# An FFT-and-GeGLU kernel: the opening of the first image in two residue halves

## The chip, the cores and the metric

The kernel runs on one core of a Trainium2 chip. The metric is the device time of one execution in microseconds (us).

## The reference

For eight images `x[b]` of 3008 x 256 the reference takes the real part of a Fourier transform along both axes and feeds each of the 24064 rows to a gated feed-forward block:

```
X = np.fft.fft(np.fft.fft(x, axis=1), axis=2).real
g = X @ w_gate;  gelu = 0.5 * g * (1 + erf(g / sqrt(2)))
out = (gelu * (X @ w_val)) @ w_out        # 256 -> 1536 -> 256
```

## The kernel before

**Numbers of the transform.** The 3008 rows are 64 x 47. For each image the kernel folds the channels (`fold_x`), multiplies by a 64-point table `G` (`a_step`, 12 of them, two of the 24 `jj` each), copies the results to `S1`, sends `S1` through DRAM to get another order on the partitions (`z_write`, `z_read`, tile `Ap`), and multiplies by 47-point tables `TP`, `TQ`, `T0P`, `T0Q` (`b_steps(b, eo, q)`: `eo` is the even or odd channel part, `q` one of four groups of eight of the 32 residues `g`). The result `Y` holds the image as columns, 1505 of them, for the even and the odd channel part. The channel transform itself is folded into the weights: `gen_w` multiplies the cast weights (`cast_w`) with a 256-point table `CW` and gives `WE`, `WOP` and `WOM` (`WOP` with a sign).

**The feed-forward part.** It runs in units. A unit is one block of 128 of the 1536 hidden channels (`fc`, twelve of them) for one chunk of columns; `CH` gives three chunks an image: columns 1024 to 1504 first (481), then 0 to 511, then 512 to 1023. An image has 36 units, and there are 288. In a unit TensorE does `val_even(u)`, `gate_minus(u-1)`, `gate_plus(u)`, `val_odd(u-1)`, six matmuls in all; ScalarE does two Gelus (`glm`, `glp`); VectorE multiplies (`plus`, and in `val_odd`). The first chunk of the first image (units 0 to 11) is of another kind than the rest (`kind` gives 0): its two products are both made by VectorE, straight from PSUM. From unit 12 on VectorE uses a row `nq` (`n_first` for image 0) and GpSimd takes part of the products. The second layer (`l2_steps`, tile `Wo_sb`) of a chunk is spread over the next chunk's units, eight matmuls a unit, so units 0 to 11 have none.

**What fills units 0 to 11.** Behind each unit's matmuls stand, in the order of the program: `gen_w` of the weight blocks 512 and 1024 (`extra`, units 0 to 7), `gen_wn` (unit 7), and `a_step` of the next image (`a_first`: step 0 in unit 4, 1 in unit 5, 2 and 3 in unit 8, two a unit in 9 to 11). They write PSUM tiles `ps_o` and `ps_d`, of which there is one buffer each; a new user waits until the copy of the one before it has been made. VectorE copies `a_step` 0, 3, 5, 7 and 9 of image 1 and makes `WOM`; ScalarE copies the others and makes `WE` and `WOP`.

**Order.** Each engine works in the order in which the program is written (`_InOrder`); nothing is moved by a scheduler. DMAs of the opening are issued by SyncE's queue, in order too. In the opening, `warm(n)` are matmuls whose result nobody reads, and `gate` is a small read that the last eight of them wait for.

**Opening, before.** Load x of image 0; build `G`; for each third of x fold, four `a_step`s, `z_write`; three `z_read`s; the tables `T`; `gen_w` of block 0; all eight `b_steps` of image 0; then unit 0.

Of the kernel before, what the change touches and what calls it, by code (L numbers as in the profile page):

```python
# [37 lines left out]
def kernel(  # L38
# [27 lines left out]
    NJ = 48  # L66
# [6 lines left out]
    CH = [(1024, NCOL - 1024), (0, 512), (512, 512)]  # L73
    MID = 24
# [26 lines left out]
    lone = const_pool.tile([128, NFC], BF16)  # L101

# [92 lines left out]
    def z_tile():  # L195
        return dram.tile([HJ, 128, C], BF16, tag="z", bufs=2, name="z")
# [50 lines left out]
    def cols_t():  # L247
        f4, f8, f16 = (col_q[:, i : i + 1] for i in range(3))
        vec.tensor_scalar(col_q, col_q, MAGIC, None, op0=ALU.add)
        vec.tensor_scalar(col_q, col_q, MAGIC, None, op0=ALU.subtract)  # L250
        vec.scalar_tensor_tensor(col_t, f4, -4.0, col_p, op0=ALU.mult, op1=ALU.add)
        vec.scalar_tensor_tensor(col_bot, f8, -2.0, f4, op0=ALU.mult, op1=ALU.add)
        vec.scalar_tensor_tensor(f8, f16, -2.0, f8, op0=ALU.mult, op1=ALU.add)
        vec.scalar_tensor_tensor(col_j, col_t, 8.0, f16, op0=ALU.mult, op1=ALU.add)
        vec.scalar_tensor_tensor(col_j, f8, 24.0, col_j, op0=ALU.mult, op1=ALU.add)
        vec.tensor_scalar(col_j, col_j, 1.0 / N2, None, op0=ALU.mult)
        for o, b0 in ((0, 0.25), (2 * N2, 0.0)):
            vec.tensor_scalar(
                _sub(quat, [[1, 2 * N2]], o), _sub(col_bot, [[0, 2 * N2]], 0),
                0.25, b0, op0=ALU.mult, op1=ALU.add)  # L260
        vec.tensor_scalar(col_k, col_t, 3.0, None, op0=ALU.is_lt)
        vec.tensor_scalar(col_w, col_k, -TWO_PI, None, op0=ALU.mult)
        vec.tensor_tensor(col_bot, col_bot, col_k, op=ALU.mult)
        vec.tensor_tensor(col_top, col_k, col_bot, op=ALU.subtract)

    TO = 4 * N2
    iota(_sub(rowt, [[2 * N2, 2], [1, 2 * N2]], 0), [[0, 2], [1, 2 * N2]], 0, 0)
    iota(_sub(rowt, [[NJ, 2], [1, MID]], TO), [[0, 2], [1, MID]], 0, 0)
    iota(_sub(rowt, [[NJ, 2], [1, MID - 1]], TO + MID), [[0, 2], [1, MID - 1]], 1, 0)
    pool.memset(_sub(rowt, [[NJ, 2]], TO + NJ - 1), 0.0)  # L270
    pool.memset(_sub(quat, [[1, NJ]], TO), 0.25)
    pool.memset(_sub(quat, [[1, NJ]], TO + NJ), 0.0)
    TG = TO + 2 * NJ
    iota(_sub(rowt, [[NG, 2], [1, NG]], TG), [[0, 2], [-11, NG]], 0, 0)
    pool.memset(_sub(quat, [[1, NG]], TG), 0.25)
    pool.memset(_sub(quat, [[1, NG]], TG + NG), 0.5)
# [59 lines left out]
    def sin_g(i):  # L336
        for h in range(2):
            act.activation(
                _sub(G, [[128, 8], [1, 64]], i * 8 * 128 + h * 64),
                _sub(reds[i], [[64, 8], [1, 64]], 0), AF.Sin, scale=col_h[h][:, :])  # L340

    def turn_g():
        for r, to, of, n, sign in ((0, 0, 0, 16, 1.0), (2, 2, 2, 16, -1.0), (1, 1, 33, 8, 1.0),
                                   (1, 33, 1, 8, -1.0), (3, 3, 35, 8, -1.0), (3, 35, 3, 8, 1.0)):
            pat = [[128, 8], [64, 2], [4, n]]
            act.activation(_sub(G, pat, 16 * 128 + to), _sub(G, pat, of), AF.Copy, scale=sign)
# [44 lines left out]
    def cast_w(f0):  # L391
        big = work.tile([128, 2, NCH, 512], BF16, tag="ev" if f0 == 1024 else "dv", bufs=2, name="wb")
        for i in (1, 0):
            wb[(f0, i)] = big[:, i, :, :]
            pool.tensor_copy(wb[(f0, i)], wst[0][:, i, :, f0 : f0 + 512])

    def gen_w(f0, i, eo, bank):
# [6 lines left out]
        if eo == 0:  # L404
            on_half(ps, act.activation(WE[:, i, fs], ps, AF.Copy))
        else:
            on_half(ps, act.activation(WOP[:, i, fs], ps, AF.Copy))
            on_half(ps, vec.tensor_scalar(
                WOM[:, i, fs], ps, col_m, None, op0=ALU.mult))

# [21 lines left out]
    def n_turn(b):  # L432
        pool.tensor_tensor(
            NA[:, :, :], _sub(Ap, [[0, 2], [C, NG]], 128), TB[:, :, :], op=ALU.mult)
# [46 lines left out]
    def z_write(b, j0, nj, eng=sync):  # L481
        if "z" not in st[b]:
            st[b]["z"] = z_tile()
        z, S1 = st[b]["z"], st[b]["S1"]
        dst = ap_replace(
            z[0:1, 0, :], ap=[[C, 128], [128 * C, nj], [1, C]], offset=z[j0, 0:1, :].offset)
        eng.dma_start(out=dst, in_=_sub(S1, [[C, nj], [1, C]], j0 * C))

    def z_read(b, third):
        z = st[b]["z"]  # L490
        src = ap_replace(
            z[0:1, 0, :], ap=[[NG * C, 32], [1, NG * C]], offset=z[8 * third, 0:1, :].offset)
        p_step = Ap[:, :, :].ap[0][0]
        dst = ap_replace(
            Ap[:, :, :], ap=[[4 * p_step, 32], [1, NG * C]],
            offset=Ap[:, :, :].offset + third * p_step)
        sync.dma_start(out=dst, in_=src)

    def b_steps(b, eo, q):
# [3 lines left out]
        def mm(gi, m1):  # L503
            def run():
                if "ps" not in box:
                    box["ps"] = ((ps_o, ps_d, ps_vh, ps_vh) if eo else (ps_vh, ps_g) * 2)[q]() \
                        if b == 0 else ps_d()
                ps = box["ps"]
                g = 8 * q + gi
                w = _sub(Ap, [[1, 1 if m1 else 128]], g * C + eo * 128)  # L510
# [4 lines left out]
                if g == 0:  # L515
                    t = T0P if even else T0Q
                    keep((pe.matmul(
                        ps[r, 0:N2], w, t[:, 0:N2], start=True, stop=True)))
                    keep(pe.matmul(ps[r, 8 * N2 : 8 * N2 + 1], w, t[:, N2 : N2 + 1],
                                         start=True, stop=True))  # L520
# [13 lines left out]
        def evac_top():  # L534
            ps = box["ps"]
            if Ys[b] is None:
                Ys[b] = Y_tile()
            copy(
                _sub(Ys[b], [[32, MID], [1, 8]], eo * YW + 8 * q),
                _sub(ps, [[1, MID], [N2, 8]], 0))  # L540

        def evac_rest():
            if Ys[b] is None:
                Ys[b] = Y_tile()
            ps, Y, g0 = box["ps"], Ys[b], 8 * q
            n2 = N2 - MID
            f = 1 if q == 0 else 0
            copy(
                _sub(Y, [[32, n2], [1, 8 - f]], eo * YW + 32 * MID + g0 + f - 1),
                _sub(ps, [[1, n2], [N2, 8 - f]], MID + f * N2))  # L550
            if q == 0:
                copy(
                    _sub(Y, [[32, n2]], eo * YW + 32 * MID + 31), ps[:, MID:N2])
                copy(
                    _sub(Y, [[1, 1]], eo * YW + NCOL - 1), ps[:, 8 * N2 : 8 * N2 + 1])

        steps = [mm(gi, False) for gi in range(8)]
        if eo == 1 and b == 0:
            steps += [mm(gi, True) for gi in range(8)]
        def evac():  # L560
            evac_rest()
            evac_top()

        return steps, evac, evac_top, evac_rest


# [11 lines left out]
    def open_unit(u):  # L578
# [3 lines left out]
        c0, n = CH[ci]  # L582
# [82 lines left out]

    def windows(b, ci):
        h = hs[(b, ci)]
        c0, n = CH[ci]
# [8 lines left out]
        if len(blocks) % 4:  # L677
# [4 lines left out]
            pool.tensor_copy(lone, h[:, :, 960:961])  # L682
# [6 lines left out]
    def l2_steps(b, ci):  # L689
# [49 lines left out]

        def store_pair(pair, t, queues):  # L740
            ns = len(pair)
            for q in range(4):
# [23 lines left out]
    for i in (1, 0):  # L766
        load_w(0, i)
    phase_g(0)
    phase_g(1)
    cols_c()  # L770
# [3 lines left out]
    pool.tensor_copy(col_k, _sub(reds[1], [[1, 1]], 0))  # L774
    for i in range(3):
# [3 lines left out]
        else:  # L779
            for t in range(NCH):  # L780
                phase_c(t)
        for k in range(4 * i, 4 * i + 4):
            a_step(0, k)
            if i == 0 and k == 3:
                z_write(0, 0, 8)
            elif i and k % 2:
                z_write(0, 2 * k - 2, 4)
        warm((5, 2, 10)[i])
    z_read(0, 0)
    z_read(0, 1)  # L790
    gate = work.tile([128, 128], BF16, tag="gate", bufs=1, name="gate")
    sync.dma_start(out=gate[:, :], in_=ap_replace(
        st[0]["z"][0:1, 0, :], ap=[[C, 128], [1, 128]], offset=st[0]["z"][0:1, 0, :].offset))
    z_read(0, 2)
    for i in (1, 0):
        load_w(512, i)
    load_x(1, 0)
    for i in (1, 0):
        load_w(1024, i)
    load_x(1, 1)  # L800
    load_x(1, 2)
    reduce_c()
    cols_t()
    pt = phase_t()
    sin_c()
    cast_w(0)
# [3 lines left out]
    gen_w(0, 0, 0, ps_g)  # L810
    gen_w(0, 0, 1, ps_vh)
    act.activation(col_f[:, :], col_p[:, :], AF.Gelu)
    warm(4)
    warm(8, gate[:, :])
    later_evacs = []
    for eo in range(2):
        for q in range(4):
            steps, evac, evac_top, evac_rest = b_steps(0, eo, q)
            for s in steps:
                s()  # L820
            if eo:
                evac_rest()
                later_evacs.append(evac_top)
            else:
                evac()
    cast_w(512)
    load_wo()
    extra = {1: [lambda: cast_w(1024)], 13: [gen_tf]}
    for n, turn in ((0, (ps_o, ps_d, ps_o, ps_d)), (1, (ps_o, ps_o, ps_d, ps_o))):
        for j, bank in enumerate(turn):  # L830
            extra.setdefault(4 * n + j, []).append(
# [15 lines left out]
    plan = [first | evens, later | evens]  # L847
    l2q, few = [], False
    for u in range(NU + 2):
# [4 lines left out]
        if u < NU:  # L854
# [4 lines left out]
            if b + 1 < B:  # L859
                for what in plan[min(b, 1)].get(i, ()):  # L860
# [7 lines left out]
                    fills += st[b + 1]["cur"][0][lo:hi]  # L868
# [13 lines left out]
        if u == 0:  # L882
# [8 lines left out]
            n_first(0)  # L891
# [21 lines left out]
        if tail:  # L913
            tail()
        if 0 < u <= NU:
# [66 lines left out]
```

## Time and profile before

| | us |
|---|---|
| median of 3 runs (range) | 631.35 (629.58 to 631.91) |
| the profiled execution: time, span | 629.75, 627.6 |
| TensorE, busy in the span | 606.0 |
| first `a_step` matmul | 8.88 |
| first `b_steps` matmul of image 0 | 25.34 |
| first matmul of unit 0 | 28.60 |
| first matmul of unit 12 | 51.62 |

A row of the timeline gives start, duration, engine, line, operation, the tile written `<-` the tiles read with their shapes, and in brackets how long the engine had been idle and what ended that. PE is TensorE, PEld its weight loads, DVE VectorE, ACT ScalarE, POOL GpSimd, SP SyncE. All instructions carry line L25, a helper's, so they are told apart by their tiles. A matmul row's duration holds its way through the array; the distance from one start to the next is what a matmul costs in a row of them.

### The profile page before, as it was taken

What the parts mean: (1) busy time and instruction counts of PE and PEld (TensorE: products, weight loads), DVE (VectorE), ACT (ScalarE), POOL (GpSimd) and SP (SyncE); (2) the same over time, 40 slices, a digit from 0 to 9 for tenths busy, and PEclk for the clock granted to TensorE, in tenths of its full rate; (3) what the DMA queues carried; (4) which work ended last, traced back from release to release, by engine and by line L of the source; (5) the groups of instructions that cost most, each with busy time, mean ns of one, the idle gap of its engine ahead of it and who ended that gap; (6) DMA issues with size and microseconds to landing.
All of it is one profiled execution on the core that took longest, in us unless ns stands there. A gap on an engine that the chain in (4) does not pass through costs nothing.

```text
span 627.6 us, 12916 instructions
## 1 busy us (share of the span) xinstructions
PE 606.0 (97%) x4522; PEld 402.0 (64%) x4580; DVE 541.5 (86%) x654; ACT 471.8 (75%) x956; POOL 449.7 (72%) x480
## 2 busy tenths in 40 slices
PE   3899999999999999999999999999999999999997
PEld 2445666766666666766667666666667666666665
DVE  7688988898888998888988898889898898999991
ACT  8687778877788777877778777887778777766662
POOL 8296987769868789687787788687885555556552
PEclk9999999999999999999999999999999999999999
DMA  8997523653237512574246533366223612222113
GB/s 311 348 283 234 153 64 113 173 185 98 76 101 218 194 49 74 177 223 121 51 119 173 190 103 74 104 208 204 56 60 93 194 45 50 60 50 52 39 47 85
DMA packets 65458, 82.39 MB, mean 131 GB/s; under 512 B 8298, under 2 KB 58986, under 8 KB 62578
## 3 DMA queue, kind: packets, MB, share of 16 engines
q1 hardware_dynamic: 63682, 80.65, 42.4%
q0 software_dynamic: 1552, 0.79, 0.9%
q8 instruction: 36, 0.59, 0.4%
q14 instruction: 28, 0.23, 0.1%
q10 hardware_dynamic: 160, 0.13, 0.1%
HBM read 45.08 MB, written 37.25 MB: 131 GB/s over the span
## 4 chain that ended last, share of the span: by engine, by line
PE 91%; DMA 3%; DVE 3%; ACT 1%; issue 1%; POOL 0%; SPq 0%; ACTq 0%; DVEq 0%; POOLq 0%
PE ps_o L25 38%; PE ps_g L25 28%; PE ps_v L25 19%; PE ps_d L25 6%; DMA xin<-in_x_dram 3%; DVE h L25 1%; DVE S L25 0%; DMA z<-S 0%; ACT glp L25 0%; DVE xf L25 0%; ACT glm L25 0%; ACT S L25 0%; POOL xf L25 0%; SPq L25 0%; DVE WOM L25 0%
## 5 line engine op out<-in xcount | busy, mean ns | idle before, releaser
L25 POOL TENSOR_TENSOR h<-glm,dv 128x1024 bf16<-128x1024 bf16 (+1 forms) x138 | 290.9, 2108 | 153.2 <-DVE dv L25 110.0
L25 PE MATMUL ps_o<-Wo_sb,h 128*128 128x256 bf16 x2136 | 277.7, 272 | 0.5 <-DVE S L25 0.3
L25 DVE SCALAR_TENSOR_TENSOR ev<-nq,WN,ps_v 128x512 f32<-128x512 bf16 (+1 forms) x276 | 202.6, 734 | 62.3 <-PE ps_v L25 43.5
L25 ACT ACTIVATE glm<-ps_g 128x512 bf16<-128x512 f32 (+1 forms) x288 | 169.4, 588 | 110.0 <-PE ps_g L25 70.8
L25 PEld LDWEIGHTS <-h 128*128 128x128 bf16 x2208 | 210.8, 97 | 54.6 <-issue 0.9
L25 ACT ACTIVATE glp<-ps_g 128x512 bf16<-128x512 f32 (+1 forms) x288 | 169.9, 590 | 9.9 <-PE ps_g L25 0.3
L25 DVE TENSOR_TENSOR h<-glp,ps_v 128x1024 bf16<-128x1024 bf16 (+2 forms) x150 | 172.9, 1153 | 4.9 <-ACT glp L25 2.7
L25 DVE SCALAR_TENSOR_TENSOR dv<-ev,ps_v 128x1024 f32<-128x1024 f32 (+1 forms) x138 | 164.8, 1194 | 0.0
L25 POOL TENSOR_TENSOR xf<-xin 128x254 bf16<-128x254 f32 x168 | 118.3, 726 | 1.8 <-DMA xin<-in_x_dram 1.8
L25 PE MATMUL ps_g<-Y,WOM 128*128 128x512 bf16 (+1 forms) x288 | 107.7, 374 | 0.3
L25 PE MATMUL ps_v<-Y,WOP 128*128 128x512 bf16 (+1 forms) x288 | 107.7, 374 | 0.0
L25 PE MATMUL ps_v<-Y,WE 128*128 128x512 bf16 (+1 forms) x282 | 105.7, 375 | 0.1
L25 PE MATMUL ps_g<-Y,WOP 128*128 128x512 bf16 (+1 forms) x278 | 103.9, 374 | 1.7
L25 PE MATMUL ps_g<-Y,WE 128*128 128x512 bf16 (+1 forms) x249 | 92.9, 373 | 0.0
L25 PEld LDWEIGHTS <-WOP 128*128 128x128 bf16 x576 | 55.7, 97 | 52.8 <-ACT WOP L25 0.4
L25 PEld LDWEIGHTS <-WE 128*128 128x128 bf16 x576 | 56.0, 97 | 30.9 <-issue 0.6
L25 ACT ACTIVATE osb<-ps_o 128x512 f32<-128x512 f32 x93 | 54.8, 589 | 17.6 <-PE ps_o L25 13.6
L25 PEld LDWEIGHTS <-Ap 128*128 128x128 bf16 (+1 forms) x561 | 40.9, 95 | 33.8 <-issue 0.2
L25 ACT ACTIVATE S<-ps_d 128x512 bf16<-128x512 f32 x80 | 47.4, 593 | 0.1
L25 PEld LDWEIGHTS <-G 128*128 128x128 bf16 x213 | 20.8, 100 | 33.2 <-issue 11.8
L25 ACT ACTIVATE Y<-ps_d 128x192 bf16<-128x192 f32 (+4 forms) x142 | 34.0, 340 | 0.5 <-PE ps_d L25 0.5
L25 PEld LDWEIGHTS <-WOM 128*128 128x128 bf16 x300 | 29.2, 97 | 4.9
(140 smaller groups left out, 262.7 us busy)
## 6 DMA issues: line engine op xcount, KB each, us to landing
out_dram<-osb SPq DMA_DIRECT2D x358, 64.0 KB
xin<-in_x_dram SPq DMA_DIRECT2D x16, 1024.0 KB
Ap<-z SPq DMA_DIRECT2D x24, 512.0 KB
xin<-in_x_dram SPq DMA_DIRECT2D x8, 896.0 KB
z<-S SPq DMA_DIRECT2D x7, 768.0 KB
z<-S SPq DMA_DIRECT2D x8, 512.0 KB
nq<-nrow SPq DMA_DIRECT2D x8, 376.2 KB
z<-S SPq DMA_DIRECT2D x11, 256.0 KB
```

What stands on the lines that cost most here:

```text
L25: return lambda *a, **k: self._tc.keep_in_program_order(call(*a, **k))
```

## The change

The 32 residues `g` are put in the order even ones, then odd ones (`G`'s columns are written in that order, `sin_g`, `turn_g`), so that partitions 0 to 63 of `S1` hold the even half and 64 to 127 the odd half. `z` becomes two tiles, and every `z_write` and `z_read` of every image two DMAs. In image 0 the even half is written and read first; only its `b_steps` (`q` 0 and 1) run before unit 0. Unit 0's chunk is now columns 0 to 511 of `Y`, in which the first 32 values of the 47 for the even residues lie; the 481 columns come second (`CH0`). The `b_steps` of the odd half (`q` 2 and 3) run as fills of units 5 to 8, each in `ps_d`, with their copies to `Y` at the end of the unit; `n_first(0)` follows unit 8. Output rows of image 0's halved chunks go out by other access patterns (`store_apart`). Around it: the matmuls of `warm` between the folds and the `gate` read are gone (13 `warm` matmuls stand where there were 29); GpSimd makes `phase_c` ahead of the folds and `cols_t` (VectorE did); VectorE casts weight block 0 (GpSimd did) and copies two of the four `gen_w` results of block 0 (ScalarE did), with both `WOM` of block 0 behind them; the next x is loaded ahead of the odd half's reads; `gen_w` of block 512 moves from units 0 to 3 to units 1, 2, 2, 3.

```diff
+    CH0 = [(0, 512), (1024, NCOL - 1024), (512, 512)]
     def sin_g(i):
-                _sub(G, [[128, 8], [1, 64]], i * 8 * 128 + h * 64),
-                _sub(reds[i], [[64, 8], [1, 64]], 0), AF.Sin, scale=col_h[h][:, :])
+                _sub(G, [[128, 8], [64, 2], [1, 32]], i * 8 * 128 + h * 32),
+                _sub(reds[i], [[64, 8], [1, 2], [2, 32]], 0), AF.Sin, scale=col_h[h][:, :])
-    def z_write(b, j0, nj, eng=sync):
+    def z_write(b, j0, nj, halves=(0, 1)):
...
+        for half in halves:
+            z = st[b]["z"][half]
+            dst = ap_replace(
+                z[0:1, 0, :], ap=[[C, 64], [64 * C, nj], [1, C]], offset=z[j0, 0:1, :].offset)
+            sync.dma_start(out=dst, in_=_sub(S1, [[C, nj], [1, C]], j0 * C, 64 * half, 64))
     def b_steps(b, eo, q):
...
-                    box["ps"] = ((ps_o, ps_d, ps_vh, ps_vh) if eo else (ps_vh, ps_g) * 2)[q]() \
-                        if b == 0 else ps_d()
+                    box["ps"] = ((ps_o, ps_d) if eo else (ps_vh, ps_g))[q]() \
+                        if b == 0 and q < 2 else ps_d()
...
+        def evac():
+            if b == 0:
+                evac_first()
+                evac_rest()
+                return
...
-    phase_g(0)
-    phase_g(1)
     cols_c()
+    for t in range(NCH):
+        phase_c(t)
...
+    phase_g(0)
+    phase_g(1)
     sin_g(0)
     sin_g(1)
     turn_g()
...
             if i == 0 and k == 3:
-                z_write(0, 0, 8)
+                z_write(0, 0, 8, (0,))
             elif i and k % 2:
-                z_write(0, 2 * k - 2, 4)
-        warm((5, 2, 10)[i])
-    z_read(0, 0)
-    z_read(0, 1)
-    gate = work.tile([128, 128], BF16, tag="gate", bufs=1, name="gate")
...
-    z_read(0, 2)
+                z_write(0, 2 * k - 2, 4, (0,))
+                if k == 7:
+                    z_write(0, 0, 8, (1,))
+                elif k == 9:
+                    z_read(0, 0, (0,))
+    warm(7)
+    z_write(0, 8, 8, (1,))
+    z_read(0, 1, (0,))
+    z_read(0, 2, (0,))
     for i in (1, 0):
         load_w(512, i)
+    z_write(0, 16, 8, (1,))
     load_x(1, 0)
+    for i in range(3):
+        z_read(0, i, (1,))
...
+    cols_t()
     reduce_c()
-    cols_t()
+    sin_c()
+    cast_w(0, vec)
     pt = phase_t()
...
-    gen_w(0, 0, 0, ps_g)
-    gen_w(0, 0, 1, ps_vh)
     act.activation(col_f[:, :], col_p[:, :], AF.Gelu)
-    warm(4)
-    warm(8, gate[:, :])
+    gen_w(0, 0, 0, ps_g, vec)
+    gen_w(0, 0, 1, ps_vh, vec)
+    for w in odd_evacs:
+        w()
+    warm(6)
     later_evacs = []
     for eo in range(2):
-        for q in range(4):
+        for q in range(2):
...
-            extra.setdefault(4 * n + j, []).append(
+            extra.setdefault(4 + j if n else (1, 2, 2, 3)[j], []).append(
...
+    second_half = {5: (0, 2), 6: (0, 3), 7: (1, 2), 8: (1, 3)}
...
+                if b == 0 and i in second_half:
+                    steps, tail, _, _ = b_steps(0, *second_half[i])
+                    fills += steps
...
         if tail:
             tail()
+            if u == 8:
+                n_first(0)
```

## The prediction

> **What bounds the kernel now.** I read the page first, then a table of busy time by stage, the chain of work that ended last, the timeline of the first 60 us, and the order in which both kernels put their instructions on each engine.
>
> ```profile
> PE 606.0 (97%) x4522; PEld 402.0 (64%) x4580; DVE 541.5 (86%) x654; ACT 471.8 (75%) x956; POOL 449.7 (72%) x480
> ```
>
> ```profile
> 28.60:51.60 23.00, 21.73 (x131) 10.50 (x131) 18.80 (x34) 19.42 (x39) 21.20 (x40) 1.00 0.84 257
> 56.00:100.00 44.00, 43.63 (x342) 28.51 (x347) 39.83 (x44) 33.59 (x74) 37.01 (x43) 1.00 0.43 134
> 100.00:600.00 500.00, 497.45 (x3696) 334.06 (x3742) 443.15 (x493) 383.88 (x773) 361.26 (x341) 1.00 0.40 117
> ```
>
> The columns are length, then PE, PEld, DVE, ACT and POOL busy, granted clock, DMA share, GB/s. From 56 us on PE is busy 99%, with 512-column matmuls 0.216 us apart, 481-column ones 0.203, 256-column ones 0.109. So what is late at unit 12 is late at the end, and what is early there is early at the end; nothing behind it can make up for it. Only the opening (0 to 28.60) and units 0 to 11 (28.60 to 51.62) decide. In the opening the chain runs through the transfers:
>
> ```profile
> 15.36 1.30 DVE S L25 x2
> 16.71 3.11 DMA z<-S
> 19.88 0.45 SPq L25
> ```
>
> The last copy of the a-steps ends at 16.66, the last write of z needs 3.11 us, the last read follows, and the first b-step starts at 25.34. In units 0 to 11 the chain goes round a loop, best seen in units 8 and 9:
>
> ```profile
> 44.35 0.37 PE L25 MATMUL ps_g<-Y,WOP 128*128 128x481 bf16 x1
> 44.82 0.57 ACT L25 ACTIVATE glp<-ps_g 128x481 bf16<-128x481 f32 x1
> 45.53 0.65 DVE L25 TENSOR_TENSOR h<-glp,ps_v 128x481 bf16<-128x481 bf16 x1
> 46.10 0.64 DVE L25 TENSOR_TENSOR h<-glm,ps_v 128x480 bf16<-128x480 bf16 x1
> 46.66 0.68 DVE L25 CAST S<-ps_o 128x512 bf16<-128x512 f32 x1
> 47.40 0.39 PE L25 MATMUL ps_o<-xf,G 128*128 128x256 bf16 x2 [0.24 <-DVE S L25]
> ```
>
> The last gate matmul, its Gelu on ACT, two products on DVE, then the copy that frees the PSUM bank, and only then may PE go on with the next user of that bank. A copy that stands behind a unit's products comes about 2.2 us after the second gate matmul. In unit 4 the same costs PE the largest wait:
>
> ```profile
> 36.68 0.75 DVE L25 TENSOR_SCALAR WOM<-ps_d,col_m 128x512 bf16<-128x512 f32 x1
> 37.48 0.38 PE L25 MATMUL ps_d<-xf,G 128*128 128x256 bf16 x2 [0.42 <-DVE WOM L25]
> 38.47 0.69 DVE L25 CAST S<-ps_d 128x512 bf16<-128x512 f32 x1
> ```
>
> **The opening, step by step.** POOL ends its column sums at 3.53; two small ones (0.45), `phase_c` (2.43) and the block of iotas (1.15) bring it to 7.56; then copy, memset, copy, memset, copy (1.30, 1.81, 0.84, 1.82, 0.79) end at 14.1. DVE's folds end at 13.67 as now, if `phase_c` does not hold up DVE's phases before 6.4 (cost 0 to 0.5, from a 0.56 us TENSOR_SCALAR beside POOL against 0.29 alone). The a-steps of the last third then start at 14.1, not behind `warm` at 14.94. The first four a-steps lie 0.42 apart, those from 12.46 on 0.22; with `warm` gone I take 0.42, so DVE's second copy ends at 16.2 (now 16.64). [...]
>
> From 16.2 DVE has `reduce_c` and `col_m` (1.65, as now), two casts of 1024, `phase_t` (1.5), then ACT's three sines (0.9), four `T0` rows (0.66). The trace has no such cast on DVE: below, twice the 0.43 us TENSOR_SCALAR of 512 less its fixed part, 0.7; above, the 1.22 us fold of 1016; I take 1.0, near POOL's 1.04 for the same shape. T is ready at 22.95. The even half of Ap is not later: about 1.05 MB of writes from 13.3 on at the 261 GB/s of the stage 13.2 to 19.1 with the last write landed 3.11 us after its issue at 16.6, and two reads of 0.26 MB behind it at 261 to 385 GB/s (0.7 to 1.0 us each), end near 22. Then DVE copies two `gen_w` results (1.3) and makes both `WOM` (1.4), and only then the even half's `Y` (0.5): 26.2. The even b-steps on PE (54 at 0.033, 1.8 us from 23) and `warm`, `gate` are covered by that. **Unit 0 starts at 26.2 instead of 28.60: 2.4 us gained**; with the cast at 0.7, 3.0, and with one POOL conflict and a cast at 1.2, 1.5.
>
> **Units 0 to 11.** Work on PE grows by 72 matmuls of 512 for 481 columns (72 x 0.0127 = 0.9 us) and by the odd half's b-steps (1.4). The waits matter more. The odd b-steps take `ps_d`, which the a-steps, `gen_w` and `gen_wn` of the same units also take, and no second-layer matmuls stand there to fill a wait. I walk the units with these durations: matmul start to its reader 0.42; Gelu 0.59, next one 0.50 later; product at 512 columns 0.69, next 0.60 (1.21 for 1024); a-step copy 0.69; WOM 0.66 to 0.75; Y copies 0.60 (0.33 for 192 elements, here 256 and 120).
>
> Unit 5: a-step 0 ends unit 4; its copy is queued behind unit 4's two products and ends 2.2 us after the a-step's start; the first odd b-step stands two matmuls into unit 5, 0.65 after: PE waits 1.55. At the unit's end a-step 1 wants the bank; the Y copy stands behind unit 5's products: Gelu 1.01 after the gate matmul, two products 1.2, Y 0.6, against 0.9 of work left on PE: 1.98. Unit 6: ACT's copy of a-step 1, 0.39; `gen_w` behind the Y copies on ACT, 1.02. Unit 7: `gen_w`'s copy 0.42; `gen_wn` behind the Y copies on DVE, 1.69. Unit 8: a-step 2 behind Y on ACT, 0.81. Unit 3: two `gen_w` in `ps_d` in neighbouring units, 0.54. Units 0, 1 and 9 to 11 keep small waits, 0.8 together. That is 9.2 us of waiting; now it is 23.0 less 20.9 of matmuls, 2.1. So 7.0 to 7.1 more, and the stage grows by 0.9 + 1.4 + 7.0 = 9.3 us.
>
> **After unit 12** the 481-column chunk stands where 512 stood: 0.9 back. Each image has two more b-step matmuls, 17 in all at 0.026: 0.4. Doubled z DMAs (six more SP issues an image, 0.36 to 0.50 each) lie beside units of 2 us, with about 10 us from the read's issue to its use; the output's changed pattern frees issues. I put both at nothing; without that cover every us that a read comes late is a us of PE in each of seven images. ACT's Y rows are written two apart from now on; ACT is busy 75%, so nothing. That nrow is written after unit 8 moves DMAs on SP: a rival below.
>
> **Sum:** -2.4 + 9.3 - 0.9 + 0.4 = +6.4 us, on the profiled execution 629.75 + 6.4 = 636.15. It lies 1.6 below the median of the runs; against 631.35 the forecast is 637.7.
>
> **Rivals.** *The waits are covered (not slower).* DVE is busy 18.8 of 23 us in units 0 to 11, and if PE ran behind the copies anyway, the bank would be free whenever it is wanted; it decides if the two waits in unit 5 stay under 0.5 us together. Then -2.4 + 0.9 + 1.4 - 0.9 + 0.4 = -0.6: 630.7; with the cheap cast 630.1. Against it: a copy behind products came 2.2 us after the gate matmul in every unit from 8 to 11. Chance 0.16.
>
> *The half writes run at half rate.* A 64-partition write of z could cost as much time as a 128-partition one of twice the bytes. At 130 GB/s the writes ahead of the last even read take 8 us and with the odd ones between and two reads Ap is whole at 26.1; b-steps and copies follow: unit 0 at 28.4, 0.2 gained, 639.9. The stores of 32 partitions speak for little of it:
>
> ```profile
> 13.20:19.10 5.90, 4.62 (x26) 2.27 (x25) 4.04 (x14) 3.66 (x8) 3.77 (x6) 1.00 0.89 261
> 570.00:575.00 5.00, 4.95 (x36) 3.42 (x36) 4.76 (x6) 3.52 (x7) 3.60 (x5) 1.00 0.22 54
> ```
>
> That is 293 GB/s for a full share of 128-partition writes and 245 for the stores, 16% less, not half. Chance 0.07. [...]
>
> *nq is late.* nrow goes out after unit 8, at 52.1; unit 12's first `ev` is due at 58.9. Now SP waits 7.7 us for nrow, with the DMA engines full. If that wait came again, with nq behind it as long as a z write (3.11), nq is there at 62.9 and unit 12 stands 4.0 us: 641.7. For the cover: from 45 to 50 us the engines now stand idle, and the loads end no later. Chance 0.07.
>
> **How the numbers follow.** The forecast has 0.70; its own range is 635.1 (waits 2 us shorter, cheap cast) to 640.6 (waits 2 us longer, 1.5 gained in the opening). The first rival (0.16) is too likely to leave out, so the range goes from 630.0 to 641.0; it leaves out the third rival and the tails. About 0.5%, 3.2 us, is what a measurement of this kernel can tell from no change. Slower by more: 0.66 of the forecast's 0.70, and the two other rivals, 0.80. Faster by more needs the first rival and an opening shorter by another 2.5 us: 0.03. Within: 0.17.
>
> **What would show it.** Right: unit 0 near 26, unit 12 near 58.5 (51.62 now), PE waiting in units 5 to 8 on DVE Y, DVE S, ACT Y and ACT S, 6 to 8 us together, DVE's share there lower than now, and PE at 99% afterwards. Wrong: unit 12 before 53; or waits on Ap by DMA ahead of unit 0; or DVE `ev` waiting for nq; or a gain or loss that grows from image to image, which I put at nothing.

## The result

The changed kernel takes 638.67 us (median of four runs, 637.78 to 639.85), the kernel before 631.56 in the same session (629.58 to 631.91): a ratio of 1.012, 95% interval 1.0093 to 1.0147. The forecast was 637.7. The profiled execution of the changed kernel is its longest, 639.85 us with a span of 638.1 (before: 629.75 and 627.6); the other three have spans of 636.0 to 637.1.

The page of the changed kernel, its line of busy time and its line of granted clock:

```profile
PE 612.5 (96%) x4581; PEld 403.5 (63%) x4581; DVE 545.4 (85%) x644; ACT 475.9 (75%) x942; POOL 454.0 (71%) x491
...
PEclk9897999999999999999999999999999999999999
```

PE is busy 6.5 us longer, and the clock is below full in the second and fourth slice, where the kernel before has a 9 in every slice. The table by stage of the changed kernel (length, busy time of PE, PEld, DVE, ACT, POOL, granted clock, DMA share, GB/s):

```profile
13.20:19.10 5.90, 5.86 (x23) 2.88 (x22) 4.11 (x11) 3.90 (x8) 5.10 (x14) 1.00 0.80 174
28.00:61.00 33.00, 25.87 (x170) 12.05 (x169) 22.32 (x33) 19.74 (x37) 22.39 (x40) 0.89 0.69 216
66.00:110.00 44.00, 43.98 (x355) 29.10 (x354) 38.72 (x45) 34.26 (x73) 39.99 (x51) 1.00 0.47 144
110.00:610.00 500.00, 500.00 (x3753) 334.18 (x3751) 442.91 (x493) 387.68 (x761) 361.21 (x340) 1.00 0.42 117
```

From 66 us on PE is as full as before; the whole difference lies ahead of it. Unit 0 begins at 26.84 (28.60 before), unit 12 at 62.72 (51.62): 1.76 us gained in the opening, 12.86 lost in units 0 to 11, 0.60 gained behind unit 12, together the 10.5 us between the two spans. The same table cut at the starts of units 0 and 12 gives for that stretch:

| | stretch | length, us | PE busy, us | granted clock |
|---|---|---|---|---|
| before | 28.60 to 51.62 | 23.02 | 21.75 | 1.00 |
| changed | 26.84 to 62.72 | 35.88 | 28.25 | 0.88 |

Of the 12.86 us, 6.50 are longer busy time of PE and 6.36 are waits (7.63 of waits, 1.27 before).

PE's waits for `ps_d`, from the timeline of units 4 to 8 (the bracket holds the idle time and what ended it):

```profile
36.84 0.38 PE L25 MATMUL ps_d<-xf,G 128*128 128x256 bf16 x2
...
38.65 0.21 PE L25 MATMUL ps_d<-TP,Ap 128*128 128x47 bf16 x2 [1.00 <-DVE S L25]
...
42.24 0.38 PE L25 MATMUL ps_d<-xf,G 128*128 128x256 bf16 x2 [1.93 <-POOL xf L25]
...
45.42 0.59 PE L25 MATMUL ps_d<-wb,CW 128*128 128x512 bf16 x2 [0.89 <-ACT Y L25]
...
50.26 0.75 PE L25 MATMUL ps_d<-CW,wb 128*128 128x1 bf16 x24 [1.52 <-DVE Y L25]
...
53.89 0.61 PE L25 MATMUL ps_d<-xf,G 128*128 128x256 bf16 x2 [0.74 <-ACT Y L25]
```

This is the chain of the forecast: a-step, odd b-steps, a-step, `gen_w`, `gen_wn`, a-step, each behind the copy of the one ahead. The second wait is put down to POOL, whose copy ended at 42.15, but DVE's copy of Y, which frees the bank, ended only 0.06 us earlier, at 42.09. In two later runs with other POOL times (`e_wn` and `e_order`) the same 1.93 us stands as DVE Y. So the bank alone is enough for it.

Two things stand there that the forecast did not have. One is a DVE copy of twelve columns. DVE's timeline has it so in the kernel before, and then in the changed one:

```profile
45.09 0.53 DVE L25 CAST WN<-WNb 128x12 f32<-128x12 bf16 x1
```

```profile
51.05 0.17 DVE L25 CAST WNb<-ps_d 128x12 bf16<-128x12 f32 x1 [0.27 <-PE ps_d L25]
51.26 4.04 DVE L25 CAST WN<-WNb 128x12 f32<-128x12 bf16 x1
55.21 0.68 DVE L25 TENSOR_TENSOR h<-glp,ps_v 128x512 bf16<-128x512 bf16 x1
```

It ends at 55.30, 0.04 us behind POOL's last fold. The other is the clock, in the table of stages cut at the times at which the grant changes:

```profile
48.79:52.20 3.41, 1.94 (x38) 1.34 (x38) 3.11 (x7) 1.01 (x2) 3.41 (x7) 1.00 0.87 120
52.20:55.62 3.42, 2.67 (x19) 1.29 (x18) 3.42 (x2) 1.95 (x5) 3.20 (x8) 0.50 0.00 1
55.62:59.03 3.41, 3.41 (x12) 1.51 (x11) 2.77 (x6) 1.79 (x3) 0.00 (x0) 0.50 0.41 113
```

The 3.41 us with the long wait are followed by 6.83 us at half, with matmuls of 512 columns 0.427 us apart instead of 0.216.

### The profile page after: what moved, and what is told of

It reads as the page before. It is cut to its first block, busy times and chain, and to the rows that moved or that the text cites. A ratio compares the mean times of both kernels' runs of the same rounds, so it can differ in the third digit from the quotient of the medians.

```text
span 638.1 us, 13004 instructions
## 1 busy us (share of the span) xinstructions
PE 612.5 (96%) x4581; PEld 403.5 (63%) x4581; DVE 545.4 (85%) x644; ACT 475.9 (75%) x942; POOL 454.0 (71%) x491
## 4 chain that ended last, share of the span: by engine, by line
PE 91%; DMA 3%; POOL 3%; DVE 1%; ACT 1%; issue 0%; SPq 0%; POOLq 0%; ACTq 0%
PE ps_o L25 38%; PE ps_g L25 28%; PE ps_v L25 19%; PE ps_d L25 6%; DMA z<-S 1%; POOL xf L25 1%; DMA wst<-in_moe_w_gate_dram 1%; DVE h L25 1%; POOL red L25 1%; SPq L25 0%; DVE S L25 0%; ACT glp L25 0%; DMA out_dram<-osb 0%; DVE red L25 0%; ACT osb L25 0%
## 5 line engine op out<-in xcount | busy, mean ns | idle before, releaser
L25 PE MATMUL ps_v<-Y,WE 128*128 128x512 bf16 (+1 forms) x288 | 108.7, 378 | 0.0
L25 PE MATMUL ps_g<-Y,WOP 128*128 128x512 bf16 (+1 forms) x288 | 108.2, 376 | 0.0
L25 PE MATMUL ps_g<-Y,WE 128*128 128x512 bf16 (+1 forms) x288 | 108.1, 375 | 0.0
L25 PEld LDWEIGHTS <-WOP 128*128 128x128 bf16 x576 | 56.0, 97 | 52.6 <-issue 0.7
L25 PEld LDWEIGHTS <-Ap 128*128 128x128 bf16 (+1 forms) x578 | 44.3, 97 | 43.2 <-issue 6.2
L25 ACT ACTIVATE Y<-ps_d 128x192 bf16<-128x192 f32 (+4 forms) x133 | 41.5, 409 | 1.5 <-PE ps_d L25 1.5
L25 PE MATMUL ps_d<-xf,G 128*128 128x256 bf16 x162 | 31.5, 277 | 2.7 <-POOL xf L25 1.9
```

What stands on the lines that cost most here:

```text
L25: return lambda *a, **k: self._tc.keep_in_program_order(call(*a, **k))
```

## The experiments

Theory 1 is the forecast's: the odd half's groups in `ps_d` make PE wait in units 5 to 8. Its rivals are the opening's transfers, POOL's late folds, the side moves and the clock; theory 2, the held DVE copy, came up on the way. Each ratio of an experiment is to the kernel before, which ran beside the experiments at medians of 629.84 to 630.22 us; the changed kernel itself was not run again beside them, so a difference of 1 or 2 us to its 638.67 says little. The starts of units in each profiled run, the time from unit 12 to the end of its span, and the median of all runs, in us:

| | unit 0 | unit 5 | unit 9 | unit 12 | units 0 to 11 | unit 12 to the end | median | ratio, 95% interval |
|---|---|---|---|---|---|---|---|---|
| before | 28.60 | 37.70 | 45.56 | 51.62 | 23.02 | 576.0 | | |
| changed | 26.84 | 37.05 | 54.71 | 62.72 | 35.88 | 575.4 | 638.67 | 1.012 (1.0093 to 1.0147) |
| `e_spread` | 27.74 | 39.19 | 48.27 | 58.16 | 30.42 | 585.1 | 642.79 | 1.0205 (1.0159 to 1.0252) |
| `e_bank` | 26.62 | 36.78 | 47.87 | 59.19 | 32.57 | 584.4 | 645.19 | 1.0244 (1.0223 to 1.0264) |
| `e_noodd` | 26.30 | 37.12 | 45.78 | 62.82 | 36.52 | 576.0 | 640.92 | 1.0165 (1.0143 to 1.0188) |
| `e_wn` | 25.05 | 36.55 | 53.47 | 59.40 | 34.35 | 575.9 | 639.75 | 1.0149 (1.0107 to 1.0192) |
| `e_spread2` | 25.84 | 36.91 | 44.87 | 52.50 | 26.66 | 579.4 | 634.46 | 1.0068 (1.0045 to 1.0092) |
| `e_spread3` | 26.53 | 37.74 | 45.69 | 52.55 | 26.02 | 582.4 | 636.0 | 1.0083 (1.0067 to 1.0099) |

All kernels here but the one before have the same transfers in the opening, and yet unit 0 begins anywhere from 25.05 to 27.74: a difference of 1 or 2 us between two profiled openings says nothing by itself.

**The odd groups spread out, and the others out of the bank** (`e_spread`; `e_bank` leaves `second_half` as it is). Both also move `gen_wn` to unit 9 and give most copies of image 1's a-steps to ACT; `e_spread` asks for `nq` behind unit 6.

```diff
-    second_half = {5: (0, 2), 6: (0, 3), 7: (1, 2), 8: (1, 3)}
+    second_half = {4: (1, 2), 6: (1, 3), 8: (0, 2), 10: (0, 3)}
-    a_first = {4: (0,), 5: (1,), ...}
+    a_first = {5: (0,), 7: (1,), 9: (2,), 10: (3,), 11: (4, 5)} | {6 + k: (k,) for k in range(6, 14)}
```

> The changed kernel with the odd half's four b-step groups in units 4, 6, 8 and 10 instead of 5 to 8 (the two of eo 1 first), and everybody else out of ps_d there: gen_w of the third weight column in ps_o, gen_wn in unit 9 in ps_o, two a-steps of image 1 before unit 9 (units 5 and 7) and the last ones up to unit 17. Nothing is left out. Theory 1 (the loss is the queue for the one bank ps_d in units 5 to 8): the waits of 1.00, 1.93, 0.89, 1.52 and 0.74 us go, small ones on ACT S of 0.25 to 0.4 in units 6, 8 and 10 stay, so 5 to 6 us less than the changed kernel: 632 to 634, unit 12 near 56. Rival 'POOL's folds are late': only the 1.93 us of the first a-steps goes, because they now come later than the folds: about 636.5. Rival 'the opening's transfers': nothing moves, 638. Rival 'the halved clock': it goes with the waits if they caused it (then another 1 to 3 us, 630 to 632) and stays if they did not.

> The changed kernel with the odd b-steps where they are (units 5 to 8, ps_d), and only the others taken out of ps_d: gen_w in ps_o, gen_wn in unit 9 in ps_o, all a-steps of image 1 from unit 9 to 18. Nothing is left out. Theory 1, in its sharper form (a bank whose copy stands behind a unit's products can be used once in two units only): the waits of a-step 1, gen_w, gen_wn and a-step 2 (1.93, 0.89, 1.52, 0.74) go, but the b-steps of units 6, 7 and 8 now wait for the Y copies of the unit before, 1.1, 0.5 and 1.1 us, so about 3.5 us less than the changed kernel, 635, and 2 us more than with the groups spread out. Rival 'the others in the bank are the whole loss': as good as with the groups spread out, 632 to 634. Rivals 'POOL' 636.5 and 'opening' 638 as there.

Units 0 to 11 became 5.5 and 3.3 us shorter, as theory 1 has it, and the whole became longer, which no theory had. The reason is what the edit itself moved: with a-steps up to unit 17 and 18 image 1's Ap is late. In `e_spread`, the timeline of PE:

```profile
85.46 0.21 PE L25 MATMUL ps_d<-T0Q,Ap 128*128 128x24 bf16 x2 [6.46 <-DMA Ap<-z]
```

The clock is at half from 83.5 to 90.4. In `e_bank` the same wait is 6.12 us. Neither total says anything on the bank, therefore, and the a-steps had no free place that far back. Inside the units both showed the long copy (4.15 and 3.94 us), in `e_bank` with 4.16 us of waiting on PE.

**The copy alone** (`e_wn`).

```diff
-        vec.tensor_copy(WN[:, :], WNb[:, :])
+        act.copy(WN[:, :], WNb[:, :])
```

> The changed kernel with one edit: the copy of the 12 columns WNb to WN is made by ACT instead of DVE. Nothing is left out. In the changed kernel DVE needed 4.04 us for it (0.53 in the kernel before), from 51.26 until POOL's folds, which stand back to back, ended at 55.3. Theory 2 (the DVE copy is held by POOL's folds, and the products of units 8 and 9 behind it are late): ACT does it in under 0.6 us, DVE goes on at 51.3, PE's waits behind unit 8 fall by 1 to 3 us: 636 to 638 for 638.7. Rival 'the wait is hidden by PE's halved clock there': the profile shows the copy short and unit 12 at the same place within 0.7 us, time within 0.7 us of the changed kernel. Rival 'ACT is held the same way': the copy takes as long there, and the Gelus behind it are late: 640 or more.

ACT needs 0.20 us for it, beside the same row of POOL's folds. Units 9 to 11 go from 8.01 to 5.93 us in the profiled runs, but the changed kernel's stood mostly at half clock. The time does not fall, 639.75 against 638.67, and no case of the expectation fits: the copy is short on ACT, and unit 12 begins 3.3 us earlier, but 1.8 of them come from the opening, which the edit does not touch. The four runs lie at 637.19, 638.35, 641.16 and 642.93, with mean clocks of 0.996, 0.997, 0.987 and 0.984, so their spread goes with the clock. The waits of 1.93, 1.51 and 0.74 us for `ps_d` are all there, and unit 4 waits 1.38 us for `wb` (0.20 in the changed kernel).

**The odd groups alone** (`e_noodd`): the odd half's b-steps and copies are left out, zeros stand in their columns.

```diff
-                    steps, tail, _, _ = b_steps(0, *second_half[i])
-                    fills += steps
+                    tail = lambda: None
```

> The changed kernel without the odd half's work in units 5 to 8: its b-steps and Y copies are left out, and POOL writes zeros into those columns of Y in the opening instead. All else stands where it is, the a-steps, gen_w and gen_wn in ps_d too, so nothing is moved to where it could be late. Theory 1 (the odd groups' hold on ps_d is what makes PE wait, and the halved clock follows the waits): besides the 1.4 us of matmuls the waits of units 5 to 8 fall from 6.6 to about 2 us and no half-clock stretch stands behind unit 4; unit 12 begins 25 to 27 us after unit 0 (35.9 in the changed kernel's profile, 34.4 in the run with WN on ACT), 629 to 631 in all. If the waits come from POOL's folds and casts and DVE's products and not from the odd groups: only the 1.4 us and some 0.5 of copies go, 636 to 637. If the 64-partition transfers of the later images cost something, it shows here as time behind unit 12 above the kernel before's 576.0 less 0.5.

Theory 1 is right up to unit 9, which now starts at 45.78 instead of 54.71, with 0.33 us of waiting left in unit 5 and 0.26 in unit 8. And then all of it is lost in one wait. Timelines of PE, DVE and POOL in this kernel:

```profile
46.65 0.38 PE L25 MATMUL ps_g<-Y,WOP 128*128 128x512 bf16 x1
56.04 0.59 PE L25 MATMUL ps_v<-Y,WOM 128*128 128x512 bf16 x1 [9.01 <-DVE h L25]
```

```profile
45.31 10.09 DVE L25 CAST WN<-WNb 128x12 f32<-128x12 bf16 x1
55.31 0.67 DVE L25 TENSOR_TENSOR h<-glp,ps_v 128x512 bf16<-128x512 bf16 x1
```

```profile
53.97 1.39 POOL L25 TENSOR_TENSOR xf<-xin 128x254 bf16<-128x254 f32 x2
55.31 0.19 POOL L25 CAST xf<-xin 128x4 bf16<-128x4 f32 x1
```

The copy comes six microseconds earlier and takes six more: it ends at 55.40, 0.04 us behind the last of POOL's folds, as in the changed kernel. (Behind the wait the clock stood at half until 61.10; an estimate from PE's 4.87 us of busy time between 55.4 and 61.1 is that this cost up to 2.4 us.) Neither case of the expectation came, 640.92 instead of 629 to 631 or 636 to 637. So the changed kernel has two chains of nearly the same length. One is the queue for `ps_d`; the other is POOL's row of folds, with DVE's copy, the products of unit 8 and PE's next `WOM` behind it. The row ends at 55.40 in the changed kernel and at 51.71 before, 3.7 us later. POOL's timeline shows why, first the kernel before, then the changed one:

```profile
33.25 2.00 POOL L25 CAST wb<-wst 128x1024 bf16<-128x1024 f32 x2
```

```profile
36.62 1.04 POOL L25 CAST wb<-wst 128x1024 bf16<-128x1024 f32 x1 [0.27 <-DMA wst<-in_moe_w_gate_dram]
42.09 1.28 POOL L25 DMA_DIRECT2D Wo_sb<-in_moe_w_out_dram  x1
```

The casts of block 1024 end at 37.66 instead of 35.25, and POOL now issues the load of `Wo_sb` in the midst of the folds. Both are moves of the change that the text on the change does not name: `load_wo` stands in unit 4 where it stood ahead of unit 0, and SP issues the load of block 1024 behind the odd half's reads, at 29.93 instead of 22.12. Who cuts one chain stands before the other.

**Both, with the a-steps in time** (`e_spread2`): groups in units 4, 6, 8 and 10, WN on ACT, all a-steps done by unit 14.

```diff
+    a_first = {5: (0,), 7: (1,), 9: (2,), 10: (3,), 11: (4, 5), 12: (7,), 13: (9,), 14: (11,), 16: (13,)}
+    a_mid = {12: (6,), 13: (8,), 14: (10,)}
```

> The changed kernel with the odd groups in units 4, 6, 8 and 10, everybody else out of ps_d in those units, WN's copy on ACT, and the a-steps of image 1 done by unit 14 and the third read of z in unit 16 (in the first form with spread groups they went on to unit 17 and PE stood 6.46 us for Ap at 85.5). Nothing is left out. Theory 1 with theory 2 (the bank's queue and the held DVE copy are the loss of units 0 to 11, 10 us more than the kernel before without a-steps and b-steps of their own weight): units 0 to 11 take 26 to 28 us (35.9 in the changed kernel, 30.4 in the first form with spread groups), no wait for Ap at 85, so 631 to 633. If the spread groups only shift the waits: units 0 to 11 at 30 or more, 635 to 637. If Ap is late again at 85: 6 us on top, 638 or more.

Units 0 to 11 take 26.66 us, as both theories together said (26 to 28), and the whole is 634.46, a ratio of 1.0068 where the changed kernel has 1.012, the best form of it that was run. It stays above the expected 631 to 633, and 0.7% slower than the kernel before. Against that kernel's profiled run the opening is 2.8 us shorter, units 0 to 11 are 3.6 longer, and what follows is 3.4 longer: six a-steps (two in the changed kernel) now stand in units 12 to 14 and wait for each other's copies (1.36, 0.38 and 0.45 us), unit 21 waits 0.64 for Ap, and 22.9 to 29.7 went at half clock. So part of what the two cuts save inside the units is only moved behind them.

`e_spread3` gives it 18 warm matmuls ahead of the b-steps and ACT for those copies.

> The second form with spread groups, with 18 warm matmuls instead of 6 ahead of the b-steps, and ACT instead of DVE copying all a-steps of image 1 but the one of unit 11. Nothing is left out. In the second form unit 12 began at 52.50 (62.72 in the changed kernel), but the clock was at half from 22.9 to 29.7 and PE waited 1.36, 0.38 and 0.45 us in units 12 to 14 on DVE's copies of S. If both are as they look: clock full at 23 to 30 (1.2 to 2 us less), 1 to 2 us less in units 12 to 14, so 631 to 632.3, within 0.3% of the kernel before. If ACT's copies stand behind its Gelus as DVE's stood behind the products: the waits stay and only the clock's part comes, 632.5 to 633.5. If the warm matmuls only shift the halved stretch to units 4 to 8, as they did in the changed kernel: 634 or more.

The clock stayed full there, and it is no faster, 636.0. Units 0 to 11 take 26.02 us, but PE waits 1.38 us for `wb` in unit 4, and in unit 21 for Ap, now 2.54 us instead of 0.64, with a halved stretch behind. Of the expected cases only "634 or more" fits, and not by its reason.

**The opening: SP's order** (`e_order`): the three even reads right behind the even writes, the odd writes behind them.

> The changed kernel with SP's order in the opening changed alone: the three reads of the even half stand right behind the even half's writes, the odd half's writes behind those reads. Nothing is left out. If the odd writes and the read issued among the even writes are what makes the even half late (last even write issued 18.15, its data ready at 16.5): that write at about 16.6, Ap's even half whole at 22.5 to 23 instead of 24.4, unit 0 at 25.5 to 26 (then DVE's copies are last), and 0.5 to 1.3 us less in all: 637.4 to 638.2. If the 64-partition writes' own rate is what makes it late: Ap at 24 again and no change. If the odd half then comes too late for unit 5: waits by DMA there and slower.

Ap comes earlier, and the whole is slower. PE's timeline:

```profile
22.70 0.19 PE L25 MATMUL ps_v<-T0P,Ap 128*128 128x24 bf16 x2 [1.45 <-DMA Ap<-z]
...
25.09 0.61 PE L25 MATMUL ps_v<-Y,WE 128*128 128x512 bf16 x1 [0.62 <-DVE Y L25]
...
30.25 0.59 PE L25 MATMUL ps_o<-wb,CW 128*128 128x512 bf16 x2 [1.38 <-POOL wb L25]
```

Ap's even half is there at 22.6 instead of 24.44. In seven profiled runs with the old order it came at 23.2 to 25.2, or 7.2 to 8.7 us behind the end of DVE's last copy of the a-steps; here it is 6.5. So the order does hold Ap back. Unit 0 at 25.09, behind DVE's copies, is early too, but `e_wn` with the old order had 25.05. And the next weights land later: POOL's casts of block 512 begin at 29.16 instead of 26.39, those of block 1024 at 36.79 instead of 35.32, and units 1 and 4 wait 1.38 and 1.35 us for them. Median 642.12 instead of the expected 637.4 to 638.2, ratio 1.0181 (1.0152 to 1.0209): slower than the changed kernel, with mean clocks of 0.987 to 0.995.

**The opening: writes of 64 partitions** (`e_half`): the kernel before, each write of z as two halves.

```diff
+        for half in range(2):
...
+            eng.dma_start(out=dst, in_=_sub(S1, [[C, nj], [1, C]], j0 * C, 64 * half, 64))
```

> The kernel before with each of its five opening writes of z, and each one of the later images, issued as two of 64 partitions, one behind the other. Nothing is left out. If only the issue counts: the last write starts 0.6 us later and lands about 0.6 to 1 us later, unit 0 at about 29.4, time 632 to 633. If a 64-partition write runs at a lower rate whatever stands beside it (in the changed kernel 174 GB/s where the kernel before had 261 in the stage 13.2 to 19.1): the writes take half as long again, Ap is whole 2 us or more later, unit 0 past 30.5, time 634 or more. If two halves side by side make up for one another, the rate is 261 again and the first case holds.

634.79, ratio 1.0076 (1.006 to 1.0093), unit 0 at 32.49 instead of 28.60: the second case. Its table by stage, and SP's timeline:

```profile
13.20:19.10 5.90, 4.39 (x23) 2.15 (x23) 4.14 (x14) 3.34 (x7) 3.74 (x7) 1.00 0.88 209
```

```profile
11.87 7.59 SPq L25 DMA_DIRECT2D z<-S  x10
```

In this stage 209 GB/s are moved with the engines as busy as in the kernel before (261 at 0.89), a rate lower by 20%, and the last half write is issued 2.1 us later, as one costs SP about 0.6 us (0.57 to 0.65 in the changed kernel) where a whole write cost 0.36 to 0.40. The `gate` matmuls begin 2.58 us later than before, little more than the issue alone explains, and take 1.31 longer at half clock; so the run does not tell how much the lower rate costs beside the longer issue. Two halves in a row did not make up for one another here.

**The opening: the clock** (`e_warm`): `warm(18)` for `warm(6)` in the changed kernel.

> The changed kernel with 18 warm matmuls ahead of the b-steps instead of 6, so that PE idles 0.2 us instead of 2.8 before Ap arrives. Nothing is left out. If the granted clock falls to half at 24.9 because PE stood idle: it stays full, b-steps and the four matmuls of unit 0 go at full spacing, unit 0 0.3 to 0.5 us earlier and unit 1 1.0 to 1.3 earlier, 637.4 to 637.9 (or less, if the later fall at 52.2 goes too). If the clock falls for another reason: it is at half there again and nothing moves.

Unit 0 at 26.25 and unit 1 at 27.31 (28.42), with full clock, about as expected; the time is 639.65 instead of the expected 637.4 to 637.9, ratio 1.0147 (1.0114 to 1.0181). In this run unit 4 waited 2.31 us for `wb`, and halved stretches followed at 38.95 to 42.36 and 52.6 to 59.4. The wait for `wb` is a third cost of the change, which no run took away alone: in the kernel before there is none in unit 4, but it is 0.20 us in the changed kernel, 1.27 in `e_noodd`, 1.38 in `e_wn` and `e_spread3`, and 2.31 in this run. What the opening gains is lost in front of these chains.

**The side moves alone** (`e_moves`): the kernel before, with POOL's and DVE's moves of the change, no gate and no warm matmuls between the a-steps, and no parity.

> The kernel before with the change's side moves alone and no parity: column sums and channel phases ahead on POOL, cols_t on POOL, the casts of the first weights and two gen_w copies on DVE, WOM deferred, the gate transfer and the warm matmuls between the a-steps left out. Nothing of the result is left out. Theory 1 (the loss comes from the odd half put into the units): within 1.5 us of the kernel before, 630 to 633, since the chain there runs through the write and the read of z; unit 0 between 27.5 and 29. Rival 'the side moves are what loses' (casts on DVE, POOL ahead of the folds, the clock without warm matmuls): 636 or more, with unit 0 after 31.

629.83, ratio 0.9986 (0.9972 to 1.0001), so the loss is not theirs. (The other order of the loads and the later `load_wo` are not among these moves.) Its whole Ap is there at 24.07 us, in `e_moves_act` below at 24.50, while the even half of the changed opening came at 23.2 to 25.2, in the changed kernel at 24.44: reading the even half first bought next to nothing, since the half writes, two odd ones among them, took longer than five whole ones (in the stage 13.2 to 19.1 the changed kernel moved 174 GB/s, `e_moves` 299). But the b-steps of `e_moves` ran at half clock:

```profile
20.43:23.84 3.41, 0.86 (x5) 0.20 (x2) 2.66 (x8) 2.37 (x6) 0.00 (x0) 1.00 0.94 318
23.84:27.25 3.41, 3.04 (x68) 2.77 (x69) 2.27 (x10) 1.14 (x4) 1.19 (x2) 0.50 1.05 415
```

`e_moves_warm` adds 13 warm matmuls, `e_moves_act` also has ACT make one of the two first WOM tiles.

> The kernel before with the change's side moves alone (as in the run of those moves), and 19 warm matmuls instead of 6 ahead of the b-steps. Nothing of the result is left out. In the run of the moves alone the b-steps began at 24.21 (25.34 in the kernel before) but took 4.2 us at the halved clock (granted 23.84 to 27.25, behind 2.92 us of waiting) where the kernel before, with its eight matmuls on the gate transfer, took 3.26. If the clock was what ate the gain: clock full there, unit 0 at 27.3 to 27.6, 0.8 to 1.2 us less than the moves alone, 628.4 to 629.2, a ratio of 0.997 to 0.998 to the kernel before. If not the clock but DVE's Y copies pace the b-steps: unit 0 stays at 28.2 to 28.5, 629.5 to 630.2.

> The side moves alone with 19 warm matmuls, and one of the two first WOM tiles made by ACT instead of DVE. Nothing is left out. In the run before, the first b-step waited 0.69 us on DVE's WOM (24.72, where Ap was there at about 24.0) and ACT stood idle from 23.1 to 25.35. If DVE's queue is the last thing ahead of the b-steps now: b-steps at 24.1, unit 0 0.5 to 0.7 us earlier, 628.3 to 628.6. If the b-steps are paced by the Y copies anyway, or Ap is whole no earlier: within 0.2 us of 629.0.

They take 629.02, ratio 0.9978 (0.9968 to 0.9988), and 628.82, ratio 0.9972 (0.996 to 0.9984): the two that beat both kernels, by 0.2 to 0.3%. For `e_moves_warm` that is the time of its first case, though unit 0 began at 27.98 and not at 27.3 to 27.6. The same two stretches of `e_moves_act`:

```profile
20.43:23.84 3.41, 3.41 (x17) 1.57 (x16) 2.31 (x8) 3.20 (x7) 0.14 (x1) 1.00 0.89 323
23.84:27.25 3.41, 3.25 (x86) 2.50 (x84) 1.97 (x10) 1.44 (x5) 0.50 (x1) 1.00 1.01 384
```

86 matmuls instead of 68 in the second. DVE's WOM was not the last thing: its wait of 0.69 us went, the b-steps waited 0.15 us for Ap and began at 24.64 (24.72), and unit 0 started 0.09 us earlier (27.89 for 27.98), the second case.

## Why the prediction was right, and where it was not

The total came out, 638.67 for 637.7, with the sign and the place right. That it came so near is partly luck. The sum of the forecast was +6.4 us. Between the medians of the two kernels lie 7.1 us, between the two profiled executions, for which the sum was worked out, 10.1: the changed kernel's is its longest run, and that of the kernel before lay below its median. Against the kernel before as it ran beside the experiments (629.84 to 630.22) the changed one is 8.5 to 8.8 us slower. Two terms were too small in the profiled run, the loss in units 0 to 11 by 3.6 us and what the opening lacks by 0.6.

- **The opening, forecast 2.4 us gained, measured 1.76.** POOL's third copy ended at 14.23 (14.1), the a-steps were 0.42 apart, the spacing that the forecast chose, and DVE's second copy ended at 16.46 (16.2). The first of these is a coincidence: `phase_c` took 3.63 us on POOL instead of 2.43, so POOL's copies and memsets began at 8.63 instead of 7.56, and then took 5.60 instead of 6.56. DVE's chain was shorter than forecast: two casts took 1.29 us, less than the lower bound of 0.7 each, and WOM was done at 24.87 instead of 25.7. The step that failed is "end near 22" for Ap: it was 24.44, and PE waited 2.77 us on that DMA. These two errors hide each other: in `e_noodd`, where the b-steps began at 24.59 and the clock stayed full, unit 0 began at 26.30, as forecast (26.2). The half microsecond that is lacking in the changed kernel is the halved clock in its b-steps (24.57 to 26.84). Ap was sized with the rate of 128-partition writes (261 GB/s) where the stage with the half writes went at 174 (162 to 212 in `e_wn`, `e_spread2`, `e_spread3`, `e_warm` and `e_noodd`, which have this opening), and the halves took about 0.6 us of SP to issue where the whole ones took 0.36 to 0.40, with an odd write and a read ahead of the last even one; with SP's order changed Ap was there at 22.6. So the second rival had part of the cause: the rate per full share was 174/0.80 = 218 (222 to 241 in those five) against 261/0.89 = 293, a fifth to a quarter less, not half.
- **The waits in units 3 to 8.** Forecast and measured, in the forecast's order: unit 3 0.54 and 0.35; unit 5 1.55 and 1.00, 1.98 and 1.93; unit 6 0.39 and 0.25, 1.02 and 0.89; unit 7 0.42 and 0.24, 1.69 and 1.52; unit 8 0.81 and 0.74. All in place, each a little shorter: 8.4 us forecast, 6.9 measured. The mechanism of the forecast, a bank whose copy stands behind other work, is what the trace shows here. DVE's share fell to 22.32 of 33 us, as was said.
- **Units 0 to 11 as a whole, forecast +9.3, in the profiled run +12.86.** The waits grew by 6.36 us where 7.0 were forecast; PE's busy time grew by 6.50 where 0.9 + 1.4 were. So the missing term is the clock: of the halved stretches 24.90 to 28.31 and 52.20 to 59.03, 8.3 us lie in these units; with matmuls 0.427 us apart there instead of 0.216, an estimate is that they cost up to half of that, which is the 4.2 us that are missing. The forecast put no price on it. The long DVE copy is a second thing that the forecast did not have, but in this run it costs nothing of its own: while PE went at half clock, it kept nobody waiting. The spans of the three other runs were 1.0 to 2.1 us shorter, with a mean clock of 0.995 to 0.997 for 0.990.
- **The cause is larger than the waits named.** "A copy behind products" and the one bank explain units 5 to 8; that their removal alone gives the time back is refuted. Without the odd groups unit 9 was 8.9 us earlier and unit 12 was not. Two chains have to be cut together, and with both cut units 0 to 11 come to 26.66 us. No form took the whole loss away: the best is still 0.7% slower than the kernel before.
- **After unit 12, forecast -0.5, measured -0.60.** The doubled transfers of the later images cost nothing that shows in the changed kernel; `e_half`, which has them too, has one wait of 0.62 us at 75.12.
- **The rivals.** The waits were not covered: the two in unit 5 came to 2.93 us. nq landed at 58.61 and was first needed at 64.1, so the third rival fell.

## What to carry to other kernels

When the trace shows a row of waits, take them away in one experiment and look at which engine is late next; here a second chain stood right behind the first, and no single cut made the kernel faster. A change that moves work to an idle-looking place must also say what that work held up there: image 1's a-steps cost more wherever they went. And a transfer that carries half the bytes by half the partitions was not a cheaper transfer here: 0.57 to 0.65 us of issue instead of 0.36 to 0.40, at a rate lower by 20 to 25%.

## What the runs showed of the hardware

**In these runs half clock came in stretches of 3.41 us, behind a partly busy PE.** In the changed kernel it lasted from 24.90 to 28.31 and from 52.20 to 59.03, once and twice 3.41 us. Two stretches of `e_wn` and what followed each:

```profile
39.40:42.81 3.41, 1.48 (x13) 0.84 (x14) 2.19 (x5) 1.18 (x3) 3.41 (x8) 1.00 0.27 107
42.81:46.22 3.41, 2.76 (x14) 0.96 (x11) 1.28 (x2) 2.04 (x5) 3.38 (x6) 0.50 0.73 233
46.22:49.63 3.41, 1.99 (x23) 0.84 (x21) 1.85 (x5) 1.71 (x3) 3.41 (x9) 1.00 1.31 228
49.63:53.04 3.41, 2.50 (x46) 1.63 (x48) 1.37 (x4) 1.94 (x5) 3.41 (x8) 1.00 0.59 82
```

With 1.48 us of matmuls the next stretch is at half, with 1.99 it is not; in the changed kernel 1.94, over half of the stretch, was followed by half. Other stretches with less than that kept the clock (1.66 us at 38.55 in the changed kernel, 1.52 at 52.80 in `e_spread`, 1.71 at 20.15 in `e_noodd`), so the busy time of one stretch does not tell by itself what follows. The stretches do not keep to the program: with the same opening the clock fell at 24.90 in the changed kernel, 24.57 in `e_bank` and 25.49 in `e_spread`, and not at all there in `e_wn` and `e_noodd`. So which wait is followed by half clock differs between runs, and a good part of the spread between runs of one kernel goes with it, as the four runs of `e_wn` show (637.19 us at a mean clock of 0.996, 642.93 at 0.984).

**DVE's copy of twelve columns lasted through many of POOL's folds.** An add or subtract of POOL's folds takes 0.71 to 0.74 us. With the new layout DVE's copy took 4.04 us in the changed kernel, 4.15 in `e_spread`, 3.94 in `e_bank` and 10.09 in `e_noodd`, ending each time 0.04 to 0.05 us behind the last fold of a long row; in the kernel before the copy took 0.53, in `e_moves` 0.72 and in `e_half` 0.25, ending 0.02 to 0.04 us behind the next pair of add and subtract of a fold. Why it ends early in the one and not in the other was not tried and stays open.
